# One DVE scaling moved a step ahead, one GpSimd marker retargeted, two loads no longer held back

## The chip, the cores and the metric

The kernel runs on one core of one Trainium2 chip. The core has five engines that run their own instruction streams in order and meet only at semaphores: PE (TensorE, matrix products), DVE (VectorE), ACT (ScalarE), POOL (GpSimd) and SP (SyncE, which here only issues DMAs). The metric is device time in microseconds of one launch.

## The reference

Attention with normalised queries and keys for 8 batches of 12 heads, 448 positions and 64 columns a head, followed by a two-layer MLP on the 768 columns of the joined heads:

```python
def rmsnorm(x, g):
    rms = np.sqrt(np.mean(x * x, axis=-1, keepdims=True) + 1e-06)
    return x / rms * g
q_n, k_n = (rmsnorm(q, g_q), rmsnorm(k, g_k))
scores = np.matmul(q_n, k_n.transpose(0, 1, 3, 2)) / sqrt(64)
attn = softmax(scores)                    # with 1e-9 added to the sum
x = np.matmul(attn, v)                    # heads joined: 3584 x 768
h = x @ w_in                              # 768 x 2048
out = gelu_tanh(h) @ w_out                # 2048 x 768, float32
```

## The kernel before, in words

**Tiling.** A batch has three chunks `c` of four heads. For each batch and chunk one load brings q and one brings k into a `raw` tile (448 KB each, four buffers for q and four for k); batch 0's chunk 0 is loaded in smaller parts. `square` and `total` give the sums of squares, `rsqrt...` the inverse roots, `normed` the scaled bf16 tiles `nrmq` and `nrmk`. These are transposed to `qT` and `kT`, on PE (`turn` and `put`) for batch 0 and for batch 1's chunks 0 and 1, by a transposing DMA (`dma_trans`, line 314) elsewhere. The product of both gains g_q and g_k is put on k alone: where PE transposes, in the copy out of PSUM (line 300); where the DMA transposes, by `gain(b, c)` (line 320), one DVE instruction over `kT[:, c]`, 128x896 bf16.

**Units.** A unit is one seventh of a chunk: four matmuls of `kT` and `qT` (line 333) into a pair of PSUM banks, then one exponential on ACT (line 337). There are 21 units in a batch, in the order of chunks. From batch 1 on three such pairs take turns, and products and MLP pairs use the same three. `key_sums` adds exponentials on DVE (lines 353 to 359); `products` multiplies them by a block of ones (sums) or by v (line 384); `turned` and `recips` make the reciprocals on DVE (lines 393, 399, 400); `quad_x` (line 408) multiplies by them and so empties the pair that holds the products.

**The loop over batches.** While batch b+1's attention runs in `attention`, PE fills its gaps with the second MLP product of an earlier batch (line 443). The 21 units come in eight groups, 0 to 7, cut at units 0, 3, 6, 9, 11, 13, 16, 18. Each group first runs the `side` entries that carry its number, then its units, then products and sums, MLP pieces and last its `behind` entries. Nothing reorders the instructions after that: on each engine they run in the order in which the Python code makes them.

**Around batch 1's attention** (the first after batch 0), the `side` list holds: the loads of batch 2 (`late_loads`, each held by a one-element DVE memset), `gain(1, 2)` in group 4, and in group 3 a marker on GpSimd, `gpsimd_waits` (line 665). The marker is a copy of one element, here of `ess[1, 0]`, the DVE's sums of exponentials of chunk 0, so GpSimd's queue stands until that sum is done. Behind it stand GpSimd's squares of batch 2: q and k of chunk 0 whole, q and k of chunk 1 in halves (line 161). DVE's totals of them (line 170) are the `behind` entries of group 4. In group 3 the DVE turns and inverts the sums of chunk 0; in group 4 PE makes chunk 0's products with v and `quad_x(1, 0)` empties them. The first unit that reads `kT[:, 2]` is unit 14, the second one of group 5.

**The start.** SP issues batch 0's chunk 0 (q's first half, k in two parts), then chunk 1 (q, k). The two loads of chunk 2 are made by `held_load` (lines 674 to 685): each first writes one element of its target with a GpSimd memset, between GpSimd's three small products of the gains (`gprod` twice, `gbf`), and these wait for the loads of g_q and g_k. The loads of batch 1's chunk 0 are SP's next.

Of the kernel before, what the change touches and what calls it, by code (L numbers as in the profile page):

```python
# [17 lines left out]
def kernel(  # L18
# [11 lines left out]
    nc = tc.nc  # L30
# [78 lines left out]
    kT = consts.tile([128, NCH, NT, 2, R], BF16)  # L109
    raws, sqs, sss, rinvs, nrms = {}, {}, {}, {}, {}  # L110
# [4 lines left out]
    def load(b, c, n, parts=1, engs=(nc.sync,)):  # L115
        t = rawqk.tile([P, 2, NT, D], F32, tag=f"raw{n}", name=f"raw{n}")
        src = {"q": q, "k": k}[n]
        raws[n, b, c] = t
        m = 2 // parts
        return [  # L120
            lambda i=i: engs[i].dma_start(
                t[:, i * m:(i + 1) * m].rearrange("p a t d -> p a (t d)"),
                src[b, 4 * c + 2 * i * m:4 * c + 2 * (i + 1) * m].rearrange(
                    "(a r) (p t) d -> (r p) a (t d)", r=2, t=NT
                ),
            )
            for i in range(parts)
        ]

    def loads(b, c):  # L130
        for n in "qk":
            for go in load(b, c, n):
                go()

    def late_loads(b, c):

        for n in "qk":
            for go in load(b, c, n):
                nc.vector.memset(raws[n, b, c][:1, 0, 0, :1], 0.0)
                go()  # L140
# [26 lines left out]
    def total(b, c, n, hs=both, ts=slice(0, NT)):  # L167
        if b not in sss:
            sss[b] = smp.tile([P, NCH, 2, 2, NT], F32, tag="ss", name="ss")
        nc.vector.reduce_sum(  # L170
            sss[b][:, seat(b, c), "qk".index(n), hs, ts], squares(b, c, n, hs, ts), axis=AX.X
        )
# [90 lines left out]
    def idle(n, w):  # L263

        for _ in range(n):
            nc.tensor.matmul(w, filler[:, :128], filler, start=True, stop=True)

    def normed(b, c, n, eng, ts=slice(0, NT)):
        if (n, b, c) not in nrms:
            nrms[n, b, c] = nrmp.tile([P, NT, 2, D], BF16, tag=f"nrm{n}", name=f"nrm{n}")  # L270
        m = ts.stop - ts.start
        root = rinvs[b][:, seat(b, c), "qk".index(n)] if eng is nc.gpsimd else roots[n, b, c]
        eng.tensor_mul(  # L273
            nrms[n, b, c][:, ts].rearrange("p t a d -> p a t d"),
            raws[n, b, c][:, :, ts],
            root[:, :, ts].to_broadcast([P, 2, m, D]),
        )
# [41 lines left out]
    def gain(b, c):  # L319
        nc.vector.tensor_scalar(kT[:, c], kT[:, c], gcol[:, 0:1], None, op0=ALU.mult)  # L320

    exs, ess, oas = {}, {}, {}
# [303 lines left out]
    load_g(1, g_k, nc.scalar)  # L626
    nc.scalar.preload_act_table_set(EXP_SET)
    loads(0, 1)

    nc.vector.memset(eps, 1e-6)  # L630
    for i in range(3):
# [28 lines left out]
    def warm():  # L660
        return oall[0][:, :S]

    def gpsimd_waits(x):

        nc.gpsimd.tensor_copy(mark, x)  # L665
# [4 lines left out]

    q_only, k_only = slice(0, 1), slice(1, 2)


    later = [(n, go) for n in "qk" for go in load(0, 2, n)]

    def held_load():
        n, go = later.pop(0)
        nc.gpsimd.memset(raws[n, 0, 2][:1, 0, 0, :1], 0.0)
        go()

    for h in range(2):
        nc.gpsimd.tensor_mul(gprod[h * D:(h + 1) * D], grow[:, 0], grow[:, 1])
    held_load()
    nc.gpsimd.tensor_mul(gbf, grow[:, 0], grow[:, 1])
    held_load()
    idle(16, warm())
    for a in range(2):
        square(0, 0, "q", nc.scalar, slice(a, a + 1))
# [42 lines left out]
    for a in range(2):  # L731
        total(0, 1, "k", slice(a, a + 1))

    side = [(1, lambda: loads(1, 0)),
            (2, lambda: loads(1, 2)),
            (7, lambda: loads(1, 1))]
# [42 lines left out]
    def transposed(b, c):  # L779
        for n in "qk":  # L780
            dma_trans(b, c, n)
# [4 lines left out]
    def normed_both(b, c, eng):  # L786
        for n in "qk":
            normed(b, c, n, eng)

    m2 = []  # L790
    for b in range(B):
        m1, side, behind, ends = [], [], [], []
        if b == 0:

            m1 = [(0, lambda: total(1, 0, "k"),
                   lambda: total(1, 2, "q"), lambda: total(1, 2, "k"),
                   lambda: rsqrt_newton(1), lambda: normed_both(1, 2, nc.gpsimd),
                   lambda: normed(1, 0, "k", nc.gpsimd)),
                  (2, lambda: total(1, 1, "q"), lambda: total(1, 1, "k"),
                   lambda: normed(1, 0, "q", nc.vector), lambda: rsqrt_last(1),  # L800
                   lambda: normed_both(1, 1, nc.vector)),
                  (4, lambda: transposed(1, 2)),
                  (6, lambda: trans(1, 0, nc.scalar)),
                  (7, lambda: trans(1, 1))]
            side += [(1, lambda: late_loads(2, 0)), (4, lambda: gain(1, 2)),
                     (2, lambda: late_loads(2, 1), lambda: late_loads(2, 2))]

            for n in "qk":
                sqs[n, 2, 1] = [
                    nrmp.tile([P, NT, 2, D], BF16, tag=f"nrm{m}", name="sq")  # L810
                    .rearrange("p t a d -> p (t a d)").bitcast(F32)
                    .rearrange("p (a t d) -> p a t d", a=1, t=NT) for m in "qk"
                ]

            side.append((3, lambda: gpsimd_waits(ess[1, 0][:1, 0, :1])))
            for c, slots in ((0, (4, 4)), (1, (4, 4))):
                for n, slot in zip("qk", slots):
                    for hs in (slice(0, 1), slice(1, 2)) if c else (both,):
                        side.append(
                            (3, lambda c=c, n=n, hs=hs: square(2, c, n, nc.gpsimd, hs)))  # L820
                        behind.append((slot, lambda c=c, n=n, hs=hs: total(2, c, n, hs)))
        elif b + 1 < B:

            m1.append((0, lambda: gpsimd_waits(ess[b, NCH - 1][:1, 0, :1])))
            for c in range(NCH):
                if b == 1 and c + 1 == NCH:
                    m1 += [(0, lambda: total(2, 2, "q")), (0, lambda: total(2, 2, "k")),
                           (0, lambda: rsqrt_last(2))]
                m1 += [(0, lambda c=c: normed_both(b + 1, c, nc.gpsimd)),
                       (4 * c + 4, lambda c=c: transposed(b + 1, c))]  # L830
            m1 += [(9, lambda: gain(b + 1, 0)), (14, lambda: gain(b + 1, 1))]
        if 0 < b and b + 2 < B:
            m1 += [(4, lambda: loads(b + 2, 1)), (8, lambda: loads(b + 2, 2))]
            for c, at in ((0, 4), (1, 9)):
                for i, (n, a) in enumerate((n, a) for n in "qk" for a in range(2)):
                    m1.append((at + i, lambda c=c, n=n, a=a: squared(b + 2, c, n, a)))
                m1 += [(at + 2, lambda c=c: total(b + 2, c, "q")),
                       (at + 4, lambda c=c: total(b + 2, c, "k"))]
            for n in "qk":
                m1.append((13, lambda n=n: square(b + 2, 2, n, nc.gpsimd)))  # L840
                side.append((0, lambda n=n: total(b + 2, 2, n)))
        if 0 < b and b + 1 < B:
            side.append((0, lambda: gain(b + 1, 2)))
        m1 = plan(*m1)
        for f in range(nf // 2 if b == 0 else nf):
            if b == 0:
                if f == 2:
                    mm1(0, 5)
                    square(1, 1, "k", nc.scalar)
                elif f > 2:  # L850
                    mm1_pair(f)
            elif f in (1, 3):
                mm1_pair(f // 2, late, b)
            elif f > 3:
                mm1(b, f)
            for fn in m1.get(f, ()):
                fn()
        m2 += m2_parts(b)
        if b + 1 == B:
            for fn in m2:  # L860
                fn()
            break
        nc.scalar.preload_act_table_set(EXP_SET)
        if b + 2 < B:
            ends.append(lambda: rsqrt(b + 2, slice(0, NCH if b else NCH - 1)))
            side += [(0 if b else 4, lambda: load_v(b + 2, 0, HP))]
            if b + 3 < B:
                side.append((1, lambda: loads(b + 3, 0)) if b else (5, lambda: late_loads(3, 0)))
        if b == 0:
            start.close()  # L870
            ps_x = ctx.enter_context(
                tc.tile_pool(name="ps_x", bufs=1, space=bass.MemoryType.PSUM))
            rounds.insert(0, ps_x.tile([128, 2, 512], F32, tag="t2", name="t2"))
        attention(b + 1, m2, 96 if b == 0 else 112, plan(*side), plan(*behind), ends)
# [30 lines left out]
```

## Time and profile before

| what | value |
|---|---|
| time, median of 3 runs | 406.08 us (405.56 to 407.76) |
| the profiled execution's own time | 405.22 us |
| its span, first to last instruction | 403.1 us |
| PE busy | 394.4 us, 98% of the span |
| ACT busy | 281.2 us, 70% |
| DVE busy | 258.5 us, 64% |
| POOL busy | 123.2 us, 31% |
| granted TensorE clock | 1.000 |

The 405.22 us hold the span and 2.1 us around it. PE's ends are modelled, so a busy PE is not one at its peak. In the timeline a row begins with its start and its duration in us from the start of the span; the brackets at its end hold the engine's idle time just before it and what ended that. "xN" says how many instructions were merged into the row. Lines are those of the kernel before.

### The profile page before, as it was taken

What the parts mean: (1) busy time and instruction counts of PE and PEld (TensorE: products, weight loads), DVE (VectorE), ACT (ScalarE), POOL (GpSimd) and SP (SyncE); (2) the same over time, 40 slices, a digit from 0 to 9 for tenths busy, and PEclk for the clock granted to TensorE, in tenths of its full rate; (3) what the DMA queues carried; (4) which work ended last, traced back from release to release, by engine and by line L of the source; (5) the groups of instructions that cost most, each with busy time, mean ns of one, the idle gap of its engine ahead of it and who ended that gap; (6) DMA issues with size and microseconds to landing.
All of it is one profiled execution on the core that took longest, in us unless ns stands there. A gap on an engine that the chain in (4) does not pass through costs nothing.

```text
span 403.1 us, 8100 instructions
## 1 busy us (share of the span) xinstructions
PE 394.4 (98%) x3321; PEld 210.1 (52%) x3321; DVE 258.5 (64%) x436; ACT 281.2 (70%) x382; POOL 123.2 (31%) x105
## 2 busy tenths in 40 slices
PE   8899999999999999999999999999999999999996
PEld 3365554555555555554555555555555545555564
DVE  5989859975796369845699257963698405990010
ACT  6995498768974887857975789748878359744301
POOL 6992407454007230183004540082301800000000
PEclk9999999999999999999999999999999999999999
DMA  8999995999415954169612948139513511110033
GB/s 281 308 223 208 199 219 200 242 234 230 91 39 118 243 107 134 41 169 281 109 41 63 263 57 217 40 86 268 75 43 78 115 24 39 50 47 24 2 78 80
DMA packets 65561, 54.07 MB, mean 134 GB/s; under 512 B 37364, under 2 KB 60532, under 8 KB 65524
## 3 DMA queue, kind: packets, MB, share of 16 engines
q1 hardware_dynamic: 53184, 41.48, 38.8%
q0 software_dynamic: 12112, 11.80, 18.7%
q8 instruction: 26, 0.43, 0.4%
q10 hardware_dynamic: 228, 0.28, 0.2%
q14 instruction: 11, 0.09, 0.1%
HBM read 45.61 MB, written 11.01 MB: 140 GB/s over the span
## 4 chain that ended last, share of the span: by engine, by line
PE 93%; ACT 2%; DVE 2%; issue 1%; DMA 1%; POOL 0%; DVEq 0%
PE o L443 37%; PE h L422 24%; PE t L473 12%; PE t L333 9%; PE t L384 8%; ACT ex L337 2%; PE o L384 1%; PE tp L291 1%; DMA rawq<-in_q_dram 1%; DVE st L393 0%; DVE ss L170 0%; DVE rb L400 0%; DVE xT L408 0%; POOL nrmq L273 0%; DVE kT L300 0%
## 5 line engine op out<-in xcount | busy, mean ns | idle before, releaser
L337 ACT ACTIVATE ex<-t,shift 128x896 bf16<-128x896 f32 x168 | 157.7, 1005 | 22.4 <-PE t L333 19.7
L443 PE MATMUL o<-wout,g 128*128 128x384 bf16 (+1 forms) x912 | 156.8, 324 | 0.0
L443 PEld LDWEIGHTS <-g 128*128 128x128 bf16 x912 | 83.6, 98 | 67.5 <-issue 18.6
L422 PE MATMUL h<-xT,win 128*128 128x448 bf16 x516 | 99.1, 352 | 0.0
L170 DVE TENSOR_REDUCE ss<-sq 128x14 f32<-128x896 f32 (+3 forms) x45 | 44.3, 998 | 48.9 <-ACT sq L159 45.9
L422 PEld LDWEIGHTS <-win 128*128 128x128 bf16 x516 | 50.5, 98 | 47.1
L428 ACT ACTIVATE g<-h 128x448 bf16<-128x448 f32 x86 | 46.7, 544 | 28.1 <-PE h L422 23.0
L453 DVE COPY osb<-o 128x384 f32<-128x384 f32 x41 | 22.7, 554 | 52.6 <-PE o L443 50.6
L333 PE MATMUL t<-qT,kT 64*64 64x448 bf16 x672 | 47.2, 359 | 2.5 <-DVE kT L300 1.0
L473 PE MATMUL t<-xT,win 128*128 128x448 bf16 x252 | 49.6, 352 | 0.0
L665 POOL COPY mark<-es 1x1 bf16<-1x1 bf16 x7 | 1.2, 177 | 146.0 <-DVE es L355 146.0
L478 ACT ACTIVATE g<-t 128x896 bf16<-128x896 f32 x21 | 18.4, 915 | 33.0 <-PE t L473 33.0
L273 POOL TENSOR_TENSOR nrmq<-rawq,rinv 128x896 bf16<-128x896 f32 (+1 forms) x21 | 34.8, 1658 | 11.9 <-DVE o L236 7.6
L473 PEld LDWEIGHTS <-win 128*128 128x128 bf16 x252 | 24.5, 98 | 22.8 <-issue 0.6
L273 POOL TENSOR_TENSOR nrmk<-rawk,rinv 128x896 bf16<-128x896 f32 x20 | 33.6, 1680 | 0.0
L333 PEld LDWEIGHTS <-kT 64*64 64x64 bf16 x672 | 17.5, 105 | 27.9 <-issue 21.5
L384 PE MATMUL t<-ex,vb 64*64 64x448 bf16 x588 | 31.6, 350 | 0.0
L451 ACT COPY osb<-o 128x384 f32<-128x384 f32 (+1 forms) x16 | 7.3, 459 | 31.5 <-PE o L443 31.5
L400 DVE STREAM_TRANSPOSE rb<-rc 128x896 f32<-128x896 f32 x24 | 26.7, 1111 | 0.8
L358 DVE TENSOR_TENSOR e<-ex 128x896 bf16<-128x896 bf16 x33 | 20.0, 607 | 9.7 <-ACT ex L337 9.4
L384 PEld LDWEIGHTS <-vb 64*64 64x64 bf16 x672 | 20.4, 107 | 11.1 <-issue 2.4
L393 DVE STREAM_TRANSPOSE st<-t 128x448 f32<-128x448 f32 x42 | 24.6, 625 | 1.3 <-PE t L384 1.3
(94 smaller groups left out, 296.7 us busy)
## 6 DMA issues: line engine op xcount, KB each, us to landing
out_dram<-osb SPq DMA_DIRECT2D x54, 192.0 KB, 2.7
rawq<-in_q_dram SPq DMA_DIRECT2D x23, 448.0 KB, 4.2
rawk<-in_k_dram SPq DMA_DIRECT2D x23, 448.0 KB, 5.1
vb<-in_v_dram POOLq DMA_DIRECT2D x7, 672.0 KB, 6.5
win<-in_moe_w_in_dram POOLq DMA_DIRECT2D x8, 384.0 KB, 11.2
wout<-in_moe_w_out_dram POOLq DMA_DIRECT2D x2, 1536.0 KB, 24.6
vb<-in_v_dram POOLq DMA_DIRECT2D x1, 448.0 KB, 9.0
qT<-nrmq SPq DMA_TRANSPOSE x19, 5.0
```

The lines of the kernel that those rows point to most:

```text
L170: nc.vector.reduce_sum(sss[b][:, seat(b, c), "qk".index(n), hs, ts], squares(b, c, n, hs, ts), axis=AX.X)
L273: eng.tensor_mul(nrms[n, b, c][:, ts].rearrange("p t a d -> p a t d"), raws[n, b, c][:, :, ts], root[:, :, ts].to_broadcast([P, 2, m, D]),)
L333: nc.tensor.matmul(sc[r * R:(r + 1) * R, a, :S], kT[rs, c, t, r], qT[b][rs, c, :, r], start=True, stop=True,)
L337: nc.scalar.activation(ex[:, t], sc[:, :, :S], AF.Exp, scale=scale, bias=shift)
L384: nc.tensor.matmul(o[r][a * D:(a + 1) * D], vb[b % 2][rs, 2 * c + a, i] if what else ones[rs], es[i][rs, a], start=(i == 0), stop=(i == n ...
L393: nc.vector.transpose(st[:, r].rearrange("p a b -> p (a b)"), oas[0][r])
L400: nc.vector.transpose(rb.rearrange("p r s -> p (r s)"), rc.to_broadcast([128, 2 * S // 32, 32]))
L422: nc.tensor.matmul(h[:, :S], win[:, c, f * 128:(f + 1) * 128], xT[b][:, c], start=(c == 0), stop=(c == HP - 1),)
L428: nc.scalar.activation(g[:, f, (b % 2) * S:(b % 2 + 1) * S], h[:, :S], AF.Gelu_apprx_tanh)
L443: nc.tensor.matmul(o, g[:, f, i * 128:(i + 1) * 128], wout[:, f, lo:hi], start=(f == 0), stop=(f == nf - 1),)
L453: nc.vector.tensor_copy(osb[:, lo:hi], o)
L473: nc.tensor.matmul(h[:, j, :S], win[:, c, f * 128:(f + 1) * 128], xT[b][:, c], start=(c == 0), stop=(c == HP - 1),)
```

## The change

Three edits.

1. The loads of batch 0's chunk 2 are issued by SP right behind those of chunk 1. `held_load` and its two GpSimd memsets are gone.
2. `gain(1, 2)` runs in group 3 of batch 1's attention instead of group 4. On DVE it now stands behind the last sum of chunk 0 (line 355) and ahead of the two transposes of the sums (line 393); before it stood between the spread of the reciprocals (line 400) and `quad_x(1, 0)` (line 408).
3. The marker in front of GpSimd's squares for batch 2 copies an element of `kT[:, 2]`, which `gain(1, 2)` writes, instead of an element of `ess[1, 0]`. So these squares wait for the scaling.

```diff
     loads(0, 1)
+    loads(0, 2)
...
-    later = [(n, go) for n in "qk" for go in load(0, 2, n)]
-
-    def held_load():
-        n, go = later.pop(0)
-        nc.gpsimd.memset(raws[n, 0, 2][:1, 0, 0, :1], 0.0)
-        go()
-
     for h in range(2):
         nc.gpsimd.tensor_mul(gprod[h * D:(h + 1) * D], grow[:, 0], grow[:, 1])
-    held_load()
     nc.gpsimd.tensor_mul(gbf, grow[:, 0], grow[:, 1])
-    held_load()
...
-            side += [(1, lambda: late_loads(2, 0)), (4, lambda: gain(1, 2)),
+            side += [(1, lambda: late_loads(2, 0)), (3, lambda: gain(1, 2)),
                      (2, lambda: late_loads(2, 1), lambda: late_loads(2, 2))]
...
-            side.append((3, lambda: gpsimd_waits(ess[1, 0][:1, 0, :1])))
+            side.append((3, lambda: gpsimd_waits(kT[:1, 2, 0, 0, :1])))
```

On each engine the other instructions keep their order.

## Prediction

> **What bounds the kernel now.** I read the page first, then the chain of work that ended last, then the order of time around the two places that the edits touch.
>
> ```profile
> PE 394.4 (98%) x3321; PEld 210.1 (52%) x3321; DVE 258.5 (64%) x436; ACT 281.2 (70%) x382; POOL 123.2 (31%) x105
> ...
> PE 93%; ACT 2%; DVE 2%; issue 1%; DMA 1%; POOL 0%; DVEq 0%
> ```
>
> PE is busy for 394.4 of 403.1 us and carries 93% of the chain: an edit elsewhere can win only a part of PE's 8.7 idle us, and loses only where it makes PE wait. Past 40 us the list of PE's own waits has one entry, 0.4 us for `quad_x` (line 408). In order of time, PE and then DVE and POOL around it:
>
> ```profile
> 64.19 1.15 PE L443 MATMUL o<-wout,g 128*128 128x384 bf16 x6
> 65.27 0.57 PE L333 MATMUL t<-qT,kT 64*64 64x448 bf16 x8
> 66.21 0.38 PE L333 MATMUL t<-qT,kT 64*64 64x448 bf16 x4 [0.37 <-DVE xT L408]
> ...
> 59.13 0.62 DVE L355 TENSOR_TENSOR es<-es,ex 128x896 bf16<-128x896 bf16 x1
> 61.04 1.18 DVE L393 STREAM_TRANSPOSE st<-t 128x448 f32<-128x448 f32 x2 [1.29 <-PE t L384]
> 62.62 1.11 DVE L400 STREAM_TRANSPOSE rb<-rc 128x896 f32<-128x896 f32 x1
> 63.66 1.50 DVE L320 TENSOR_SCALAR kT<-kT,gcols 128x896 bf16<-128x896 bf16 x1
> 65.08 1.08 DVE L408 TENSOR_TENSOR xT<-t,rb 128x896 bf16<-128x896 f32 x1
> ...
> 61.59 1.68 POOL L161 TENSOR_TENSOR sq<-rawq 128x896 f32<-128x896 f32 x1 [1.59 <-DMA rawq<-in_q_dram]
> 63.23 1.68 POOL L161 TENSOR_TENSOR sq<-rawk 128x896 f32<-128x896 f32 x1
> ```
>
> To be seen: unit 15 (66.21) stands 0.37 us because its PSUM pair is emptied by `quad_x`, which ends at 66.16; ahead of that is the scaling, 1.50 us long beside GpSimd's squares. DVE had idled 1.29 us before 61.04, waiting for PE; GpSimd idled until 61.59 for a load and not for the marker (59.82).
>
> For the start I read the rates by microsecond:
>
> ```profile
> 6.00:7.00 1.00, 0.17 (x3) 0.04 (x2) 1.00 (x4) 0.94 (x5) 0.67 (x3) 1.00 1.04 396
> 7.00:8.00 1.00, 0.94 (x14) 0.72 (x14) 0.98 (x2) 0.78 (x3) 1.00 (x2) 1.00 0.98 305
> 8.00:9.00 1.00, 0.74 (x8) 0.30 (x6) 0.83 (x5) 0.90 (x4) 1.00 (x1) 1.00 1.03 362
> ```
>
> The last two columns are the DMA engines' share and GB/s: full (near 1.00) from 3 us on, with one dip in the rate at 7 to 8.
>
> **The change, part by part. The scaling (edit 2).** It leaves its place between 63.73 (the spread of the reciprocals done) and 65.08. `quad_x` then starts at the later of 63.73 and the end of PE's products with v, 62.74 + 1.52 = 64.26; as elsewhere (products end 76.25, `quad_x` starts 76.30) 0.05 later: 64.31, and it ends at 65.39. Units 13 and 14 hold PE until 65.27 + 0.57 = 65.84, so unit 15 no longer waits: **-0.37 us**, all of it on PE. Not more, since past that PE has no gap here.
>
> In its new place the scaling follows line 355, which ends at 59.75, and costs 0.44 us (18 of the 19 scalings run in some 445 ns; the median is 445, the maximum 1503 is this one). It ends at 60.25, inside the 1.29 us in which DVE waits for PE until 61.04: 0 on the path, with 0.8 us to spare. The cover goes if its transposed k is not there: that DMA was issued at 43.58 and took 13.9 us, so it landed at 57.5, 2.3 us ahead. Without GpSimd beside it the scaling also gives back 1.06 us of DVE time.
>
> What is late next? ACT: its exponential of unit 16 waits 0.30 us for PE at 69.18, behind an output copy that ends at 68.88, so ACT can follow by 0.30 to 0.32 us and then waits another 1.00 at 72.09: PE keeps its 0.37. DVE: the six totals (4.17 us from 66.08) move to 65.39 but stay behind GpSimd's last square, which ends at 66.81 + 1.82 = 68.63: last total about 69.5 (70.25 before), the next sum ends at 70.1, and the transpose of the sums, which PE releases at 70.64 - 0.37 = 70.27, is not held.
>
> **The marker (edit 3).** One 0.18 us copy stays one. GpSimd stands behind it until 60.25 + 0.2 instead of 60.0. Queued behind are the squares, and the totals wait for them; the first square waits for batch 2's q until 61.59 either way, so 1.1 us of cover: 0. The squares could run up to 0.1 us sooner, as the halves that met the scaling took 1.97 us and the next two 1.82; nobody waits for that.
>
> **The loads (edit 1).** Two memsets (0.09 us each) leave GpSimd. The normalisation at 6.38, on the chain, starts 0.33 us after the memset before it. Its other condition, ACT's inverse root, ends at 6.03 + 0.21 = 6.24. At 18.59 the same pair shows 0.08 us from ACT's end to GpSimd's start, so 6.32 is possible: between 0 and -0.06 us, and I take **-0.06**, by that row, since what follows (PE's transposes at 7.48, the copies, the first exponential at 8.98) waits in a row.
>
> On SP the two loads move from 5.83 and 6.31 to about 3.2 and 3.9 (the second needs the semaphore of the first load of all, landed at 3.9), and the two of batch 1's chunk 0 behind them from 6.75 and 7.26 to between 4.3 and 5.1 (the last needs g_k's semaphore, seen by 5.09). The next, 7.84, still waits for its buffer, free at 7.43: at most 0.3 us sooner. Nobody waits for any of these four: GpSimd squares chunk 2 at 12.34 and 13.99, and it landed at 9.2 and 10.5 (issue plus time to landing); batch 1's chunk 0 is squared from 20.25. The bytes ahead of them set the pace: the loads issued at 2.19, 2.70, 5.83 and 6.31 landed at 6.9, 8.0, 9.2 and 10.5, one after the other, 1.1 to 1.3 us apart, which is 448 KB at 350 to 400 GB/s. So earlier issue wins only the dip at 7 to 8, (370 - 305) GB/s for 1 us or 0.2 us of DMA time, where no engine waits for DMA: 0. It may lose: the loads of chunk 1 (needed at 7.38 and 9.02, landed 6.9 and 8.0) now have others behind them at once. Lowest loss 0, if the queue is served in turn. Highest: all four loads share the rate and land together at 10.5; q is then 3.1 us late, and GpSimd's squares, DVE's totals, the inverse root at 11.67 and ACT, which is over 0.9 busy there, move with it: +3.1. The four landings in a row lie at the first end: **0**.
>
> Here the Trainium skill, page "DMA: Bandwidth & Descriptors", section "Queues, rings and completion order", says that each DMA engine takes descriptors of one ring in order, but that a later one may finish writing before an earlier one. The landings here agree with the first half, and by it the sum stays as it is; by the second half alone it would move towards the upper end.
>
> **Sum.** -0.37 - 0.06 = -0.43 us on the profiled execution: 405.22 - 0.43 = 404.8. The median of the three runs, 406.08, lies 0.86 above that execution; on that scale 405.65, which I give as 405.7. A change of 0.5% (2.0 us) is about what a measurement of this kernel can tell from none, so this is "same".
>
> **Rivals.**
> - *The stall only changes its cause.* Products and their ends are modelled; if `quad_x` in truth waits for the products until 64.7 or for DVE's queue, unit 15 still waits. For it: 64.26 leaves only 0.45 us. Against it: in batch 2 two sums of 1.2 us together stand in the scaling's place, from 110.58 to 111.74, and PE shows no wait there. Time: 406.0.
> - *Chunk 1 lands late (slower).* Priced above. It is one mechanism, sharing among queued loads; it outweighs the gain once q lands 0.9 us later (7.8) or k 1.5 us later (9.5). For it: the load of 6.75, queued deep, landed at 12.55, 2.0 us behind its forerunner and not 1.3, so a deep queue delays by some 0.7; that alone brings q to 7.6 and costs 0.2. In full: 405.7 + 3.1 = 408.8, half way 407.2.
> - *The scaling stalls DVE.* Transposed k lands after 60.6; up to 61.5 that is hidden, since `quad_x` may start at 64.7 without holding PE, and from 61.9 on the change loses, 1 us per us. Against it: 57.5 in the trace, 4 us away. At 64: 408.
> - *The start gains.* If full DMA queues brought everything forward by the 0.2 us of the dip, and PE with it: 405.5. Against it: neither GpSimd nor DVE waits for a load between 6.4 and 40 us.
>
> **How the numbers follow.** Forecast 0.62; stall changes its cause 0.15; chunk 1 late 0.13 (half of that above 408.1); scaling stalls 0.03; start gains 0.07. The forecast and its neighbours lie within 405.5 to 406.0, but runs of the same kernel spread from 405.2 to 407.8, so the range is 404.4 to 407.3: it drops the upper half of "chunk 1 late" and the ends of the spread. Slower by over 0.5%: 0.06 from chunk 1, 0.01 from the scaling and 0.03 of spread, 0.10. Faster by over 0.5%: no case but spread, 0.06. Same: 0.84.
>
> **What would show it.** Right: the scaling about 0.45 us long just before 60.3, no wait of PE for line 408, `quad_x` from 64.3, unit 15 right behind unit 14; GpSimd's first square of batch 2 released by its load; the loads of chunk 2 issued at 3 to 4 us and GpSimd's square of chunk 1's q still at 7.3 to 7.4. Wrong: a wait for rawq or rawk on GpSimd before 12 us, the inverse root later than 11.7, or DVE waiting for transposed k near 60 us.

## The result, and the profile after

| | before | after |
|---|---|---|
| median of 14 runs each, us | 406.31 (405.08 to 407.76) | 404.54 (404.34 to 405.89) |
| ratio after / before | | 0.9966, 95% interval 0.9952 to 0.9980 |
| profiled execution, us | 405.22 | 405.40 |
| its span, us | 403.1 | 403.6 |

The change is faster by 0.34%, 1.4 us by that ratio (1.8 us between the two medians), and the interval leaves out 1. The first trap is in the lower half of the table: the profiled execution of the changed kernel is *longer* than that of the kernel before. One trace of each kernel would have told the story the wrong way round. *Span* is always the time from the first to the last instruction of an execution.

Unit 15's stretch in the profiled execution of the changed kernel, PE, then DVE, then GpSimd, in order of time:

```profile
65.31 1.15 PE L443 MATMUL o<-wout,g 128*128 128x384 bf16 x6
66.38 0.76 PE L333 MATMUL t<-qT,kT 64*64 64x448 bf16 x12
...
60.25 0.62 DVE L355 TENSOR_TENSOR es<-es,ex 128x896 bf16<-128x896 bf16 x1
60.79 0.45 DVE L320 TENSOR_SCALAR kT<-kT,gcols 128x896 bf16<-128x896 bf16 x1
62.16 1.18 DVE L393 STREAM_TRANSPOSE st<-t 128x448 f32<-128x448 f32 x2 [0.92 <-PE t L384]
65.42 1.09 DVE L408 TENSOR_TENSOR xT<-t,rb 128x896 bf16<-128x896 f32 x1 [0.57 <-PE t L384]
...
62.18 1.68 POOL L161 TENSOR_TENSOR sq<-rawq 128x896 f32<-128x896 f32 x1 [0.71 <-DMA rawq<-in_q_dram]
```

The scaling takes 0.45 us instead of 1.50, inside DVE's wait for PE. Units 13 to 15 run as one row of twelve matmuls without a wait, and `quad_x` now waits for PE's products. All of this stands 1.1 us later than before, though, and that came in at the start. ACT's inverse root of chunk 1 there (line 195 is its first instruction), before and after:

```profile
11.67 0.32 ACT L195 ACTIVATE lg<-ss,eps 128x28 f32<-128x28 f32 x1
```

```profile
12.77 0.32 ACT L195 ACTIVATE lg<-ss,eps 128x28 f32<-128x28 f32 x1 [0.77 <-DVE ss L170]
```

And GpSimd's square of chunk 1's q, first in the kernel before, then in a second execution of it, and then in the changed kernel:

```profile
7.38 1.68 POOL L161 TENSOR_TENSOR g<-rawq 128x896 f32<-128x896 f32 x1
```

```profile
8.99 1.68 POOL L161 TENSOR_TENSOR g<-rawq 128x896 f32<-128x896 f32 x1 [1.42 <-DMA rawq<-in_q_dram]
```

```profile
8.62 1.68 POOL L161 TENSOR_TENSOR g<-rawq 128x896 f32<-128x896 f32 x1 [0.98 <-DMA rawq<-in_q_dram]
```

To be seen: in both kernels the first square of chunk 1 may have to wait for its load. The execution of before that the prediction was built on was one in which it didn't.

### The profile page after: what moved, and what is told of

It reads as the page before. It is cut to its first block, busy times and chain, and to the rows that moved or that the text cites. A ratio compares the mean times of both kernels' runs of the same rounds, so it can differ in the third digit from the quotient of the medians.

```text
span 403.6 us, 8096 instructions
## 1 busy us (share of the span) xinstructions
PE 393.4 (97%) x3321; PEld 209.8 (52%) x3321; DVE 257.7 (64%) x436; ACT 281.0 (70%) x382; POOL 123.0 (30%) x103
## 4 chain that ended last, share of the span: by engine, by line
PE 94%; ACT 2%; DMA 2%; POOL 1%; DVE 0%; SPq 0%; issue 0%
PE o L443 38%; PE h L422 24%; PE t L473 12%; PE t L333 9%; PE t L384 8%; ACT ex L337 2%; DMA rawq<-in_q_dram 2%; PE o L384 1%; POOL g L161 1%; PE tp L291 1%; SPq L617 0%; PE os L384 0%; DVE st L393 0%; DVE ss L170 0%; PE o L266 0%
```

## The experiments

Theory A was the prediction's: the start is fixed, the gain is at unit 15. Theory B: the landing of chunk 1's loads differs from execution to execution in both kernels. Others were formed on the way. The short names in the expectations are: *held* for the kernels whose loads of chunk 2 wait for a GpSimd memset, *not held* for those with edit 1.

### The parts alone

The kernel before against itself:

> The kernel before, unchanged, timed against itself: ratio 1.000, its interval holds 1. Theory A (the start is fixed, the gain lies at unit 15): chunk 1's q lands at 6.9 to 7.2 us again and GpSimd's first square starts at 7.4. Theory B (the landing of chunk 1's loads differs from one execution to the next in both kernels, and the median of before, about 1 us above its first profiled execution, holds a late start in most runs): this execution shows the inverse root of chunk 1 either at 11.7 or about 1 us later, and its span follows by the same amount (403.1 or about 404.2 us).

The scaling and the marker alone:

```diff
-            side += [(1, lambda: late_loads(2, 0)), (4, lambda: gain(1, 2)),
+            side += [(1, lambda: late_loads(2, 0)), (3, lambda: gain(1, 2)),
...
-            side.append((3, lambda: gpsimd_waits(ess[1, 0][:1, 0, :1])))
+            side.append((3, lambda: gpsimd_waits(kT[:1, 2, 0, 0, :1])))
```

> Edits 2 and 3 alone, loads still held. In the two profiles the stretch from unit 0 of batch 1 to the end of group 5 became 0.55 us shorter. Theory A: the whole measured gain (1.4 us, ratio 0.9966) that is not the loads': ratio 0.9986, 0.55 us less than before, with the start as in before. Theory B: the same 0.55 us, and the rest, about 0.85 us, belongs to the loads. Theory C (the scaling carries all of the gain): ratio 0.9966.

The loads alone:

```diff
     loads(0, 1)
+    loads(0, 2)
...
-    held_load()
     nc.gpsimd.tensor_mul(gbf, grow[:, 0], grow[:, 1])
-    held_load()
```

> Edit 1 alone, scaling and marker as before. Theory A: no change, ratio 1.000. Theory B: earlier issue changes how often the start is late; ratio 0.998, about 0.85 us less in the median, with single executions that are 1 us above the others. Theory C: 1.000 or above, since the profile of the changed kernel shows chunk 1's q landing at 8.55 instead of 6.9 us and the start 1.1 us later.

The changed kernel again:

> The changed kernel as it is, a second execution in the trace: ratio 0.9966 again. Theory B: the execution in the trace is of the common kind (span 402.7 us), with chunk 1's q landing before 7.4 us, GpSimd's first square at 7.4 and the inverse root of chunk 1 near 11.7, or of the late kind as the first one was (8.55, 8.62 and 12.77; span 403.6). Theory A: it looks like the first, and the common 402.7 comes from somewhere else.

| kernel | ratio to before (95%) | median, us | profiled span, us | inverse root of chunk 1 starts at |
|---|---|---|---|---|
| before, again | 0.9987 (0.9967 to 1.0008) | 405.31 | 404.9 | 13.14 |
| scaling and marker alone | 0.9992 (0.9967 to 1.0016) | 405.65 | 403.8 | 12.98 |
| loads alone | 0.9966 (0.9947 to 0.9986) | 404.57 | 403.6 | 12.17 |
| all of the change, again | 0.9969 (0.9947 to 0.9991) | 404.45 | 402.4 | 11.56 |

The loads alone reach the measured ratio. Timed twice more, they gave 0.9974 (0.9951 to 0.9996) and 0.9985 (0.9955 to 1.0016), so the size is uncertain and the last interval even holds 1; the 35 runs together have a median of 404.73 us, against 405.96 for the 105 runs of before that were timed beside all these kernels. Theories A and C, which both had the loads at 1.000 or above, fall. The scaling can't be told from nothing, nor from the 0.56 us (0.9986) of the next section: its interval holds both. B's picture of the executions holds in part: the same kernel before gave a span of 403.1 with the inverse root at 11.67 and one of 404.9 with it at 13.14, which is 1.47 of the 1.8 us.

### Three terms make up a span

With the unit-15 wait and the wait for w_out (below) read off each trace, every traced execution at full clock fits one sum: span = 390.9 + start of chunk 1's inverse root + wait at unit 15 + wait for w_out. The constant is from the first execution of before (403.1 - 11.67 - 0.56). A wait counts with 0.2 us more than its row shows, because four matmuls take 0.38 us after a wait and 0.19 in the stream.

| execution | root | unit 15 | w_out | sum | span |
|---|---|---|---|---|---|
| before, again | 13.14 | 0.2 | 0.8 | 405.0 | 404.9 |
| scaling and marker alone | 12.98 | 0 | 0 | 403.9 | 403.8 |
| loads alone | 12.17 | 0.6 | 0 | 403.7 | 403.6 |
| after | 12.77 | 0 | 0 | 403.7 | 403.6 |
| after, again | 11.56 | 0 | 0 | 402.5 | 402.4 |

In "before, again" PE's twelve matmuls of units 13 to 15 take 0.94 us and not 0.76, which is the 0.2. The full-clock traces that came later fit too, within 0.2 us. So in an execution like the first of before, moving the scaling is worth 0.56 us and not 0.37. Why that doesn't show in the medians was the next question, and what lies outside the span the third: time less span is 2.11 us (2.05 to 2.18) in the executions with held loads, the scaling alone among them (2.10), and in the mean 1.78 to 1.80 (1.74 to 1.86) in the kernels without, but for one made to test this (below). That is 0.3 us of edit 1's gain in each execution.

### w_out's landing, from both sides

The second execution of the kernel before shows PE waiting for a load that the prediction never named, the second half of w_out:

```profile
63.46 1.14 PE L443 MATMUL o<-wout,g 128*128 128x384 bf16 x6 [0.62 <-DMA wout<-in_moe_w_out_dram]
```

In the first execution this load, issued at 31.37 with 29.7 us to landing, came at 61.1. Its issue, its landing and PE's row there, in which the third product is the first that needs it:

```profile
31.37 1.20 POOL L655 DMA_DIRECT2D wout<-in_moe_w_out_dram  x1
wout<-in_moe_w_out_dram POOLq DMA_DIRECT2D x1, 1536.0 KB, 29.7
60.85 1.47 PE L443 MATMUL o<-wout,g 128*128 128x384 bf16 x8
```

PE took that product at 61.18. There was next to no slack, and no row of the list of waits said so. The kernels with nothing held have no more of it as a rule: from landing to first use it is 0.02 us in the loads alone, 0.13 in the changed kernel's second execution and 0.8 in its first, which starts late; 2.3 us, in the kernel without edit 3 below, is the most. Two experiments: the second half in two DMAs, so that PE's first eight products of it need only the first (on the changed kernel, and on the loads alone), and the loads held longer than ever.

```diff
-    def w_out_part(i):
-        nc.gpsimd.dma_start(
-            wout[:, :, i * HD:(i + 1) * HD],
-            moe_w_out[:, i * HD:(i + 1) * HD].rearrange("(f p) d -> p f d", p=128),
-        )
+    def w_out_part(i, n=1):
+        m = nf // n
+        for j in range(n):
+            nc.gpsimd.dma_start(
+                wout[:, j * m:(j + 1) * m, i * HD:(i + 1) * HD],
+                moe_w_out[j * m * 128:(j + 1) * m * 128, i * HD:(i + 1) * HD]
+                .rearrange("(f p) d -> p f d", p=128),
+            )
...
-            lambda: w_out_part(1)),
+            lambda: w_out_part(1, 2)),
```

> The changed kernel, but the second half of w_out comes in two DMAs (blocks f 0 to 7 and 8 to 15), so that PE's first eight products of that half no longer wait for its last bytes. In the traces so far that landing (60.96, 61.1, 61.5, 61.66, 63.4 us) lies within 0.0 to 1.0 us of the moment PE needs it, and once behind it. Theory D (the landing of w_out is the floor under the undisturbed executions): the lowest spans fall from 402.5 to 402.2 or less and no execution waits for w_out; ratio 0.995 to 0.996. Theory B (only chunk 1's landing counts): nothing moves, spans 402.4 to 402.8 with a third of the executions near 403.8, ratio 0.9967.

> The same split of w_out on the kernel with edit 1 alone (scaling and marker as before). Theory D: with the floor gone the scaling shows, and this kernel lies 0.3 to 0.56 us above the one with the scaling moved. Theory E (the wait at unit 15 depends on where a GpSimd square happens to stand when the scaling comes, and is absent in most executions): no difference between the two, spans 402.5 to 402.8 for most.

```diff
     loads(0, 1)
-    loads(0, 2)
...
     normed(0, 0, "q", nc.gpsimd, t_first)
+    for n in "qk":
+        for go in load(0, 2, n):
+            nc.gpsimd.memset(raws[n, 0, 2][:1, 0, 0, :1], 0.0)
+            go()
```

> The changed kernel, with chunk 2's loads held longer than in before: their memsets stand behind GpSimd's normalisation, so they are issued at about 7.5 and 8.0 us. Theory B in its first form (queued loads in front of nobody help chunk 1): chunk 1 is not slowed by others behind it, the start is late less often, spans 402.6 as the rule. Theory D (what counts is the DMA stream kept full, as w_out's landing near 61 us follows from it): the queue runs dry for about 1 us, w_out lands up to 1 us later, PE waits for it, lowest span 403.0 to 403.5, ratio about 1.000. Time less span: 2.11 if the held loads make it.

| kernel | ratio to before (95%) | median, us | lowest span | profiled span |
|---|---|---|---|---|
| all of the change, w_out split | 0.9974 (0.9952 to 0.9995) | 404.90 | 402.4 | 404.0 |
| loads alone, w_out split | 0.9991 (0.9963 to 1.0019) | 405.39 | 402.5 | 404.7 |
| all of the change, loads held to 7.7 and 8.2 | 1.0054 (1.0024 to 1.0085) | 408.73 | 403.8 | 404.9 |

Splitting lowers nothing: w_out is not the floor under the best executions, and theory D fails there. Its other sign, the loads alone 0.3 to 0.56 us above the changed kernel, fits the medians (0.5 us), but the two intervals overlap widely, so it decides nothing. w_out was not split on a kernel with its loads held as before, which is where a trace had shown the wait. Holding longer fails B's first form badly. GpSimd's first square indeed had no wait in that trace, the inverse root came early (11.91), and the kernel lost 4.2 us in the median. The windows of the start (last two columns: the DMA engines' share, GB/s) and PE's row at w_out, both of the kernel with the loads held longer:

```profile
7.00:8.00 1.00, 0.74 (x10) 0.55 (x11) 1.00 (x3) 0.78 (x3) 0.97 (x4) 1.00 0.41 156
8.00:9.00 1.00, 0.74 (x12) 0.40 (x8) 0.81 (x5) 0.97 (x4) 1.00 (x1) 1.00 0.44 50
9.00:10.00 1.00, 1.00 (x12) 0.33 (x9) 1.00 (x3) 0.93 (x2) 1.00 (x2) 1.00 0.67 213
```

```profile
63.68 1.14 PE L443 MATMUL o<-wout,g 128*128 128x384 bf16 x6 [2.08 <-DMA wout<-in_moe_w_out_dram]
```

The DMA engines' share fell to between 0.41 and 0.67 from 7 to 10 us, and 54 us later PE stood 2.08 us. In the changed kernel's second execution the same windows are full:

```profile
7.00:8.00 1.00, 0.94 (x14) 0.65 (x12) 0.92 (x2) 0.83 (x3) 1.00 (x2) 1.00 1.04 376
8.00:9.00 1.00, 0.74 (x7) 0.30 (x6) 0.93 (x5) 0.90 (x4) 1.00 (x2) 1.00 1.04 400
9.00:10.00 1.00, 1.00 (x11) 0.39 (x9) 1.00 (x2) 1.00 (x2) 1.00 (x2) 1.00 1.05 401
```

And in the second execution of before there is a small hole, of the same kind as the one at 7 us of the first:

```profile
7.00:8.00 1.00, 0.83 (x12) 0.64 (x13) 0.75 (x2) 0.36 (x2) 0.57 (x1) 1.00 0.84 222
8.00:9.00 1.00, 0.43 (x6) 0.13 (x3) 0.74 (x3) 1.00 (x4) 0.01 (x1) 1.00 0.99 371
```

By 14 us the DMA engines had finished packets of 4.28, 4.22 and 4.11 MB in the first held executions (before twice, scaling alone), 3.58 MB where the loads were held longer, and 4.34 to 4.46 MB in all executions that hold nothing. Between the changed kernel's second execution and the one held longer, the gap of 0.8 MB at 14 us is still 0.8 MB at 61 us (14.8 and 14.0 MB by the rates): there the bytes not moved at 8 us were still missing. For holes as small as those of before this is not shown. Scaling alone had moved the least of the three, and PE didn't wait for w_out in it. (Seven of the twelve executions held longer also ran at a granted clock under 0.997; the five others have spans of 403.8 to 404.9, still 1 us or more above the changed kernel's 402.7. The one trace is at 0.999, and the sum above gives 405.1 for its 404.9.)

### Does GpSimd's instruction count make the 0.3 us outside?

```diff
+    scrap = consts.tile([1, 2], F32)
+    nc.gpsimd.memset(scrap[:, 0:1], 0.0)
     nc.gpsimd.tensor_mul(gbf, grow[:, 0], grow[:, 1])
+    nc.gpsimd.memset(scrap[:, 1:2], 0.0)
```

> The changed kernel with two one-element memsets back on GpSimd at the old places, but on a tile that nobody reads, so that they hold no load back. The time less the span is 2.11 us in the kernels with held loads and 1.79 us in those without. If the two GpSimd instructions make this difference: 2.11 again. If the loads' being held makes it: 1.79. The span stays at 402.5 to 404.

Time less span came out between both: 1.95 us in the mean (1.89 to 2.07, nine executions). Held longer, it was 2.09. So about half of the difference goes with two GpSimd instructions that do nothing, the rest with the holding; by what road, no trace shows. The ratio of this kernel, 0.9971 (0.9947 to 0.9995), is that of the change; the one trace had a lowered clock (0.992, span 406.1).

### When does the scaling cost anything?

> Edit 1 alone once more, for a second execution in the trace. Four executions with the scaling in its old place show it 1.5 to 1.8 us long, yet the undisturbed executions of these kernels have the same span (402.5 to 402.8) as those with the scaling moved. Theory E (whether the scaling waits depends on where GpSimd's squares stand): an execution of 402.5 to 402.8 us shows the scaling at 0.45 to 0.8 us and no wait of PE for line 408. Theory F (the wait is always there and such executions start earlier): the scaling is 1.4 to 1.8 us long, PE waits 0.3 to 0.6 us, and the inverse root of chunk 1 comes at 11.1 or earlier, 0.4 to 0.5 before the earliest seen (11.56). If the execution is a late one (403.5 and above), both remain.

> The kernel before, a third execution in the trace, for the same question and for w_out: Theory E and F as for edit 1 alone. In the first two executions w_out landed at 61.1 and 63.4 and PE needed it at 61.18 and 62.84; theory D says that an execution of this kernel whose bytes moved by 14 us are 4.2 MB or less shows PE waiting for it.

> Edit 1 alone, a third execution in the trace; the last one began with a lowered clock and could not tell the two theories apart by its span. Theory E: an execution of 402.4 to 402.8 us shows the scaling at 0.45 to 0.8 us and no wait of PE for line 408, with the inverse root of chunk 1 at 11.5 to 11.7. Theory F: the scaling is 1.4 to 1.8 us long, PE waits 0.3 to 0.6 us, and the inverse root comes at 11.1 or earlier.

The three executions, with the scaling in its old place (inverse roots at 12.80, 12.93 and 12.23; the first ran at a granted clock of 0.87 in its first 20 us, so its span says nothing), beside those from above:

| execution | span | scaling, us | GpSimd's square before it ends | scaling ends | wait at unit 15 |
|---|---|---|---|---|---|
| before, first | 403.1 | 1.50 | 64.91 | 65.16 | 0.56 |
| before, second | 404.9 | 1.80 | 66.69 | 66.94 | 0.2, PE late by w_out |
| loads alone, first | 403.6 | 1.53 | 65.44 | 65.69 | 0.6 |
| before, third | 404.3 | 1.40 | 66.08 | 66.33 | 0.5 |
| loads alone, third | 403.3 | 1.12 | 65.10 | 65.34 | 0.2 |
| loads alone, w_out split | 404.7 | 1.80 | 66.51 | 66.76 | 0.8 |
| loads alone, second | 405.8 | 0.75 | about 67.4 | 67.68 | none |

GpSimd's two half squares and then DVE in the second execution of the loads alone; the first half ends at about 67.4:

```profile
66.51 1.97 POOL L161 TENSOR_TENSOR sq<-rawq 128x448 f32<-128x448 f32 x2
...
65.90 1.11 DVE L400 STREAM_TRANSPOSE rb<-rc 128x896 f32<-128x896 f32 x1
66.93 0.75 DVE L320 TENSOR_SCALAR kT<-kT,gcols 128x896 bf16<-128x896 bf16 x1
67.61 1.08 DVE L408 TENSOR_TENSOR xT<-t,rb 128x896 bf16<-128x896 f32 x1
```

The scaling ends 0.24 to 0.25 us after GpSimd's square each time, wherever it began: it waits for the square's end. So its price is a matter of phase, from nothing to 0.8 us in seven executions, and theory E holds as far as that. But each of the six at full clock lost 0.2 to 0.8 us; the one without a loss is the one with the lowered clock. The Trainium skill, page "SBUF — State Buffer", section "Who interferes with whom", calls the port pair that VectorE and GpSimd share an exclusive lock, in which the later of the two blocks until the other's instruction is over; these rows agree with it. That the best executions with the scaling unmoved (spans of 402.5) have no wait at all was not caught in a trace, so it stays argued: by the sum above, a wait would need an inverse root before 11.56, the earliest seen. The third execution of before moved 4.34 MB by 14 us and PE didn't wait for w_out; the bound of 4.2 MB that theory D gave for this kernel was not reached, and so not tried.

### The marker

The change without edit 3:

```diff
-            side.append((3, lambda: gpsimd_waits(kT[:1, 2, 0, 0, :1])))
+            side.append((3, lambda: gpsimd_waits(ess[1, 0][:1, 0, :1])))
```

> Edits 1 and 2 without edit 3: the marker reads the sum of chunk 0 again. By the prediction GpSimd's first square waits for batch 2's q until about 61.5 to 62.2 in any case, and the scaling is done by then: scaling 0.45 us, spans as with all three edits, ratio 0.997. If the marker is needed: a square starts before the scaling ends, and the scaling takes 1 us or more.

Ratio 0.9980 (0.9956 to 1.0004), median 404.62 us. Scaling 0.45 us, from 59.71; GpSimd's first square began at 60.30, after a load that here came early:

```profile
59.71 0.45 DVE L320 TENSOR_SCALAR kT<-kT,gcols 128x896 bf16<-128x896 bf16 x1
59.85 0.34 POOL L666 COPY mark<-es 1x1 bf16<-1x1 bf16 x1 [14.62 <-DVE es L355]
60.30 1.68 POOL L161 TENSOR_TENSOR sq<-rawq 128x896 f32<-128x896 f32 x1
```

Here the load was no cover: the square started at 60.30, 0.14 us after the scaling's end at 60.16, and the copy of one element took 0.34 us beside the scaling instead of 0.18. The marker ended at 60.19, 0.03 us after the scaling, so edit 3 is insurance of a small width, and its effect on the time is below what these runs tell.

## Why the prediction was right or wrong

The time, 404.54, lies in the range, near its lower edge (404.4), and the direction was right; the size was not: -0.43 us was forecast and 1.4 measured. The gain came with the edit that was priced at -0.06 in all. That the time still lies in the range owes to the room left for the spread between runs, not to the sum; that much is luck.

- **The scaling, -0.37.** The steps came as forecast: 0.45 us in the new place, inside DVE's wait, `quad_x` released by PE's products, unit 15 behind unit 14. In the first execution of before it is worth 0.56, as the refill of PE's stream was left out. What failed is that it was counted in full for every execution: it depends on where GpSimd's squares stand (0.2 to 0.8 us in the full-clock traces). Alone the edit measured 0.9992 (0.9967 to 1.0016), and the changed kernel's 26 runs have a median 0.2 us below the 35 of the loads alone; neither tells 0.4 us from nothing.
- **GpSimd's memsets, -0.06.** Nothing. The normalisation starts 0.34 to 0.36 us after the start of ACT's inverse root in eight executions, with memsets (6.03 to 6.38) and without (5.93 to 6.27). The profile's name for the releaser was not the cause.
- **The loads, 0.** Wrong, and this was most of the miss: edit 1 alone gave ratios of 0.9966 to 0.9985 where nothing was forecast. Two things were put at nothing. One is the time outside the span, which fell by 0.3 us. The other is the dip at 7 to 8 us, seen and written off "where no engine waits for DMA": PE depends on that stream 54 us later, with next to no slack (61.1 against 61.18), and a deeper hole there made it wait 2.08 us. That the dip of before costs anything is not shown, though: PE waited for w_out in one of the four traces with loads held as before and in none of the nine with nothing held. The rival "the start gains" (0.07) named the right edit, but its 0.2 us is too little and its road, an earlier start, is not shown either.
- **"Chunk 1 lands late"** was a rival of one kernel against the other. In fact it happens in both: the landing of its q made GpSimd wait in three of the four traced executions with loads held as before, and in seven of nine with nothing held (among these the two at a lowered clock at the start). The prediction's account of before held the one start without it. The traced executions are no fair sample of how often: two of those nine have spans up to 403.0 us, and 58% of all runs of these kernels do.
- **The median.** The forecast carried the 0.86 us by which the median lay above the profiled execution over to the new kernel as a constant. That distance is the spread of the starts and waits, and it didn't stay: the changed kernel's median lies 0.86 below its profiled execution.

Over all runs at a granted clock of 0.997 and above, 33% of 117 executions with loads held as before have a span up to 403.0 us and 26% one above 404.25; of 97 executions with nothing held it is 58% and 5%. Shown is that edit 1 alone makes the kernel faster, by about 1.2 us in the medians of all runs, and that about 0.3 us of it lie outside the span. How the rest, some 0.9 us of the median span (403.8 for before, 402.9 for the loads alone), divides between earlier starts and fewer waits for w_out stays open: the traces are too few, and chunk 1's late landing is in both kernels.

## What to carry to other kernels

A profile without a wait for a load is not proof of slack: compare the landing of each large load with the moment of its first use. Where the DMA engines are busy without a break for 60 us, a hole of 0.8 MB in their work at 7 to 10 us was paid 54 us later by the load that had no slack, so a queue is to be kept filled there. And where the median lies well away from the profiled execution, find out what varies between executions before adding up terms of a few tenths of a us.

## What was not expected of the hardware

- One slow share of a transfer holds the whole load back. In the second execution of before, the 768-byte packets of k's second part end at 4.6 us in the median, the last at 7.4 us (4.5 and 5.2 in the first), and the load landed at 7.7 instead of 5.5. Chunk 1's q, queued behind, landed at 8.9 instead of 6.9; that the slow share is the reason is not shown, as q came as late as 8.5 in the changed kernel, where the last of these packets ended at 6.0. The Trainium skill, page "DMA: Bandwidth & Descriptors", section "Why a DMA increments its semaphore by 16 and not by 1", says that a DMA's engines finish independently and that only the full count means that all has landed; the packets agree with it. What slows the one share, no run shows.
- The time outside the span moves by 0.16 us in the mean with two GpSimd instructions of 0.09 us each, and by 0.3 us with them and the held loads.
- With the loads held longer, seven of twelve executions had a granted clock of 0.992 to 0.996 in the mean; among the 26 of the changed kernel none was below 0.998. The one trace with the wait of 2.08 us is at 0.999, so what lowers the clock in the others is not shown.
